# All seven probability slots of a pair by DMA transpose from the eleventh pair on, the scale of v taken in its cast, and half-folded squares on GpSimd

## The chip, the core and the metric

The kernel runs on one NeuronCore of a Trainium2 chip. The core has five engines that run their own instruction streams: TensorE (PE, matrix products; its weight loads, PEld, overlap it), VectorE (DVE), ScalarE (ACT), GpSimd (POOL) and SyncE (SP, which issues the DMAs here). They meet only in semaphores. Operands lie in SBUF; matrix products go to PSUM, eight banks of 512 f32 per partition. The metric is the device time of one execution in microseconds (us).

## What is computed

Attention with RMS-normalised q and k over 8 batches of 12 heads (448 positions, 64 features a head), and then a gated feed-forward block with a three-tap convolution along the sequence:

```python
q_n, k_n = rmsnorm(q, g_q), rmsnorm(k, g_k)
scores = q_n @ k_n.T / sqrt(64)
attn = exp(scores - max(scores)); attn = attn / (sum(attn) + 1e-9)
x = (attn @ v), heads side by side            # 8 x 448 x 768
h = relu(x @ w_in)                            # 768 -> 1024
c = conv3(h, conv_w)                          # along the sequence, per feature
out = (h * sigmoid(c)) @ w_out                # 1024 -> 768
```

## The kernel before

**Pairs.** The unit of attention is a pair of heads (`n`, 0 to 47, six to a batch). Its two heads of 448 rows make 896 query rows, cut into seven **slots** of 128; `SLOTS` gives the order in which they are done, and `GROUPS` joins them for `scores`. A pair passes these steps, each a small function that issues one or a few instructions:

- `load_k`, `load_q` (lines 329 to 338), `square` (340), `square_sum` (349), `rsqrt` (362, nine small steps for two pairs at once), `apply_rms` (396), `qk_transpose` on PE (408), and `qk_hi`, `qk_lo` (419, 427), which split a value into two f16 parts, high and rest.
- `scores` (532) on PE with three f16 products, `soft_max` (545, the row maximum, DVE), `soft_exp` (551, ACT, with the row sums).
- The probabilities have to be turned, so that the keys lie on the partitions. There are two ways. **By PE**: `p_transpose` (582, four transposes of f32) into PSUM and `p_evac` (589, ACT or DVE) out of it into an f32 part of the tile `PT`. **By DMA**: `p_hi` (560) and `p_lo` (568) split the slot into two f16 parts in a buffer `ph`, and `p_turn` (575) is one DMA transpose of both into an f16 part of `PT`. `nd(n)` (516) says how many slots go by DMA: none for the pairs 0 to 7, four (slots j = 0 to 3) for the others.
- `v_load` (461), `v_bound` (466, the largest absolute value), and once for a batch `v_max` to `v_scale` (476 to 493), a power of two by which v is scaled. `v_scaled` (631) multiplies the tile v by it in place. Where slots go by DMA, `v_hi` and `v_lo` (637, 640) split v into two f16 parts.
- `pv` (652) multiplies: the f32 part with four passes over k for both heads (line 660), and the f16 part with three products (line 669). `pvs(n)` lists its pieces.
- The row sums: `sum_step` (596), `sum_transpose`, `sum_evac`, `sum_store` to DRAM and `sum_load` back, spread over 64 partitions; `x_scale` (674) multiplies the PV by them; `x_hi`, `x_lo` split the result for the next product.

**The feed-forward block** of a batch: `in_part` (736) on PE, `in_relu`, `in_conv` (three), `in_tanh`, `in_gate`, `in_hi`, `in_lo`, `in_carry`, and `out_part` (798) on PE, `out_evac`, `out_store`. It is worked into the attention of the next batch, so that PE has products to do while a pair waits for its softmax.

**Order.** Nothing is scheduled on the chip. `plan_*` give each step a due time (`at`), `needs` (915) what it must follow, and `options` (1167) the engines that may do it, with a cost. A list scheduler (1269 to 1396) walks through these and writes out a single order; each engine runs its share of that order from first to last. The constants `PH` (20) shift due times and set how patient a step is with its second engine. `SHARED` (1316) names steps whose DVE form is costed higher when POOL is busy. SP issues all DMAs in one order, loads, sums, turns and stores alike.

**Buffers** (`BUFS`, 104): three of `ph`, two of `PT`, three of `e` (the exponentials), twelve of `x`, eight of `v`.

Of the kernel before, what the change touches and what calls it, by code (L numbers as in the profile page):

```python
# [9 lines left out]
F16 = mybir.dt.float16  # L10
# [10 lines left out]
    T0=18.19, N0=5, T=16.2, ti=26.477, si=4.987, so=6.734, hop=0.568, beta=0.028, wi0=-41.512,  # L21
    wi1=117.871, wo0=38.32, wo1=142.628, cw=-29.146, p_evac=1.158, p_hi=2.093, p_lo=3.44,
    p_rms=1.831, p_v=1.927, p_x=0.005, p_g=2.46, p_relu=0.434, p_cv=1.228, p_qz=1.0, p_ev=8.316,
    sp=0.107, nbulk=5, p_rs=0.005, p_sq=0.882, p_w=0.5, v0=-5.896, dg=2, n1=8, sw=0, pvs=2,
    ct=1.5, p_vs=0.938, p_ph=0.39, p_pl=0.493,
# [23 lines left out]
def tile_attention_moe(ctx: ExitStack, tc, q, k, v, g_q, g_k, w_in, conv_w, w_out, out):  # L49
# [298 lines left out]

    def square_sum(n):
        m = duo(n)[0]  # L350
        nc.vector.tensor_reduce(  # L351
            old("st", m)[:, 0, n - m].rearrange("p i s -> p (i s)"),
            old("sq", n).rearrange("p i h t d -> p (i h t) d"), axis=AX.X, op=ALU.add,
        )
# [273 lines left out]
    def pvs(n):  # L628
        return (*range(0, NB, PV_STEP), *(range(NB, NB + 3) if nd(n) else ()))

    def v_scaled(n):
# [1 line left out]
        elementwise(on["v_scaled", n]).tensor_scalar(  # L633
            v, v, old("vsc", n // NP)[:PB, 1:2], None, op0=ALU.mult
        )
# [793 lines left out]
```

## Time and profile before

| | |
|---|---|
| median of three runs | 978.2 us (975.87 to 981.03) |
| the profiled execution | 978.28 us, span 976.5 us |
| mean granted TensorE clock | 0.962 |
| q1, all DMAs that the kernel issues | 259664 packets, 109.82 MB, 52.1% of 16 engines' span |
| p_turn | 160 DMA transposes |

The page's first part gives busy time, share of the span and number of instructions of each engine; its second part cuts the span into 40 equal slices, each digit being tenths of the slice (9 is 90% or more). A group's row reads: line, engine, operation, written tile <- read tiles, shapes, count | busy time, mean ns of one | idle time ahead of it and what ended it. In a row of the timeline the first number is the start in us and the second the duration; matrix products are pipelined, so the start of the next row tells more than the duration. Many helper functions issue for several steps (line 77 a copy or cast, line 81 a scaled one on ACT, line 89 an operation on two tiles): there, the tile's name tells the step.

### The profile page before, as it was taken

How to read it: one execution, taken by the hardware profiler on the slowest of the kernel's cores; microseconds unless marked ns; L12 is line 12 of the kernel's file. 1: busy time of each engine (PE TensorE's matmuls, PEld its weight loads, DVE VectorE, ACT ScalarE, POOL GpSimd, SP SyncE). 2: the span in 40 equal slices, each digit the busy share in tenths (PEclk: the TensorE clock that was granted, in tenths of full speed). 3: DMA queues.
4: the chain of work that ended last, by engine and by line, in shares of the span. 5: the costliest groups of instructions: out<-in, count | busy, mean ns of one | idle time of the engine just before them, and what ended most of it. 6: DMA issues, size and time to landing. Idle time of an engine off the chain costs nothing.

```text
span 976.5 us, 18886 instructions
## 1 busy us (share of the span) xinstructions
PE 893.8 (92%) x6590; PEld 522.6 (54%) x6590; DVE 777.3 (80%) x1349; ACT 680.4 (70%) x1564; POOL 660.1 (68%) x723
## 2 busy tenths in 40 slices
PE   1777688978999799999999999999999999999988
PEld 0344344545656366655665566556665665556545
DVE  6999979899689967699789977898889966992540
ACT  3678667776666777679688776788788776785331
POOL 2489868886687758498688767587778864772120
PEclk9788669998999999999999999999999999999999
DMA  9945423343773677555765667446684565244001
GB/s 215 247 105 148 126 57 76 64 101 71 155 160 75 107 125 149 116 110 103 153 133 122 125 133 148 102 92 139 144 163 92 109 148 100 51 94 107 17 16 50
DMA packets 259759, 111.02 MB, mean 114 GB/s; under 512 B 220928, under 2 KB 256080, under 8 KB 259664
## 3 DMA queue, kind: packets, MB, share of 16 engines
q1 hardware_dynamic: 259664, 109.82, 52.1%
q8 instruction: 52, 0.85, 0.3%
q14 instruction: 43, 0.35, 0.1%
HBM read 56.65 MB, written 11.18 MB: 69 GB/s over the span
## 4 chain that ended last, share of the span: by engine, by line
PE 49%; DVE 12%; POOL 6%; issue 3%; ACT 3%; DMA 1%; SPq 0%; POOLq 0%; ACTq 0%; DVEq 0%
POOL ph L89 1%; POOL gring L89 1%; POOL sq L89 1%; DMA PT<-ph 1%; DVE st L351 1%; DVE ph L89 1%; POOL x L89 1%; POOL st L386 1%; DVE c_(1_4_3520 L763 0%; POOL st L375 0%; DVE carry L788 0%; PE m_('o'_7_0_0_12066 L812 0%; PE m_('o'_5_3_0_10563 L812 0%; PE m_('o'_3_3_0_7531 L812 0%; PE m_('o'_1_3_0_4495 L812 0%
## 5 line engine op out<-in xcount | busy, mean ns | idle before, releaser
L742 PEld LDWEIGHTS <-wi 128*128 128x128 f16 x1152 | 108.7, 98 | 99.8 <-issue 16.6
L812 PEld LDWEIGHTS <-gring 128*128 128x128 f16 (+1 forms) x1056 | 101.3, 100 | 66.4 <-issue 16.9
L89 POOL TENSOR_TENSOR sq<-qkf,st 112x512 f32<-112x512 f32 x80 | 96.0, 1214 | 2.8 <-ACT wi L254 1.0
L89 POOL TENSOR_TENSOR x<-rB,x 128x448 f16<-128x448 f32 x48 | 57.2, 1191 | 49.3 <-ACT x L77 39.5
L633 POOL TENSOR_SCALAR v<-v,vsc 112x512 f32<-112x512 f32 x42 | 72.0, 1718 | 17.8 <-DVE vsc L186 16.1
L543 PEld LDWEIGHTS <-qT 64*128 64x128 f16 x864 | 32.5, 96 | 71.1 <-issue 55.5
L351 DVE TENSOR_REDUCE st<-sq 112x16 f32<-112x1024 f32 x48 | 58.0, 1209 | 3.2 <-ACT sq L345 2.4
L669 PEld LDWEIGHTS <-vp 112*64 112x64 f16 x960 | 51.1, 110 | 9.7 <-issue 7.8
L441 POOL COPY qz<-qT 64x128 f16<-64x128 f16 x90 | 37.4, 416 | 25.8 <-DVE qT L432 23.1
L89 POOL TENSOR_TENSOR vp<-v,vp 112x512 f16<-112x512 f32 x38 | 46.3, 1219 | 8.9 <-ACT vp L77 6.6
L345 ACT ACTIVATE sq<-qkf 112x1024 f32<-112x1024 f32 x33 | 34.9, 1059 | 4.5 <-DMA qkf<-in_q_dram 4.5
L89 POOL TENSOR_TENSOR sq<-qkf 112x1024 f32<-112x1024 f32 x15 | 30.1, 2005 | 4.5 <-PE t_('qk'_7_0_1418 L412 2.3
L471 DVE TENSOR_REDUCE vacc<-v 112x1 f32<-112x512 f32 x48 | 32.2, 671 | 0.3
L77 ACT CAST vp<-v 112x512 f16<-112x512 f32 x36 | 22.2, 618 | 11.4 <-PE m_('v'_18_4614 L669 3.4
L600 DVE TENSOR_SCALAR rsum<-rsum 128x7 f32<-128x7 f32 x48 | 20.8, 432 | 8.2 <-ACT e_(29_6_7231 L555 1.5
L812 PEld LDWEIGHTS <-carry 128*64 128x64 f16 x192 | 20.2, 114 | 10.8 <-issue 4.1
L375 POOL TENSOR_SCALAR st<-st 112x32 f32<-112x32 f32 (+1 forms) x53 | 19.1, 360 | 10.0 <-DVE st L388 4.2
L386 POOL TENSOR_TENSOR st<-st 112x32 f32<-112x32 f32 (+1 forms) x25 | 10.1, 406 | 22.5 <-DVE st L381 19.4
L812 PEld LDWEIGHTS <-wi 128*128 128x128 f16 (+1 forms) x192 | 19.6, 102 | 9.3 <-ACT wi L77 0.5
L788 DVE COPY carry<-gring 128x128 f16<-128x128 f16 x32 | 19.2, 599 | 5.8 <-POOL gring L89 5.8
L543 PEld LDWEIGHTS <-qz 128*128 128x128 f16 x144 | 14.1, 100 | 16.5 <-issue 6.4
L89 DVE TENSOR_TENSOR sq<-qkf,st 112x512 f32<-112x512 f32 x16 | 22.7, 1424 | 0.0
(3733 smaller groups left out, 3134.2 us busy)
## 6 DMA issues: line engine op xcount, KB each, us to landing
qkf<-in_k_dram SPq DMA_DIRECT2D x48, 224.0 KB
qkf<-in_q_dram SPq DMA_DIRECT2D x48, 224.0 KB
v<-in_v_dram SPq DMA_DIRECT2D x48, 224.0 KB
rB<-rd SPq DMA_DIRECT2D x96, 112.0 KB
wo<-in_moe_w_in_dram SPq DMA_DIRECT2D x12, 512.0 KB
gring<-in_moe_w_out_dram SPq DMA_DIRECT2D x16, 384.0 KB
PT<-ph SPq DMA_TRANSPOSE x160
rd<-rT SPq DMA_DIRECT2D x48, 3.5 KB
```

The source lines that it names most:

```text
L77: (nc.scalar.copy if e == "ACT" else elementwise(e).tensor_copy)(dst, src)
L89: elementwise(e).tensor_tensor(dst, a, b, op=op)
L345: nc.scalar.activation(sq, old("qkf", n), AF.Square)
L351: nc.vector.tensor_reduce(old("st", m)[:, 0, n - m].rearrange("p i s -> p (i s)"), old("sq", n).rearrange("p i h t d -> p (i h t) d"), axi ...
L441: e.tensor_copy(z[HALF[h], :, HALF[h]], old("qT", n)[HALF[h], :, t0 : t0 + 64])
L471: nc.vector.tensor_reduce(old("vacc", b)[:PB, i : i + 1], old("v", n).rearrange("p h t d -> p (h t d)"), axis=AX.X, op=ALU.max, apply_abso ...
L543: nc.tensor.matmul(ps[u][:, :S], lhs, kt[r, w], start=(i == 0), stop=(i == 2))
L600: nc.vector.tensor_scalar(r, r, 1e-9, None, op0=ALU.add)
L633: elementwise(on["v_scaled", n]).tensor_scalar(v, v, old("vsc", n // NP)[:PB, 1:2], None, op0=ALU.mult)
L669: nc.tensor.matmul(ps[HALF[h], out[h]], v[:, w, h, k], pt[:PB, a, k, col[h]], start=(i == 0 and k == 0), stop=(i == 2 and k == NB - 1),)
L742: nc.tensor.matmul(ps[:, :S], wi[:, wl, c, fc * P : (fc + 1) * P], old("x", b * NP + c)[:, xl], start=(i == 0), stop=(i == 3 * NP - 1),)
L812: nc.tensor.matmul(ps[p0 : p0 + m, :NO2], g, wo[:, wl, fc, half * NO2 : (half + 1) * NO2], start=(i == 0), stop=(i == 3 * NFC - 1),)
```

## The change

Five things are done together.

1. `nd(n)` is 0 for the pairs 0 to 9 and 7 for all others. From the eleventh pair on every slot goes through `p_hi`, `p_lo` and `p_turn`; `p_transpose` and `p_evac` are left to the first ten pairs. `pv` is then three f16 products 448 columns wide, with no f32 part. 266 turns take the place of 160. `ph` has four buffers and `x` eleven.
2. `v_scaled` is gone. `v_hi` multiplies by the scale in its cast, `v_lo` is one DVE instruction (product and subtraction), and in the first ten pairs `x_scale` multiplies by the scale too.
3. `square_fold`: in the first 15 pairs POOL adds the upper halves of the 64 squares of a row to the lower halves, and `square_sum` reduces 32 instead of 64.
4. Order: `p_turn` of a pair's first slot follows the pair before, `qk_transpose` follows the scores of two pairs earlier, and between some DMAs (`LOOSE`) the scheduler keeps the order but counts no waiting time. The due times are worked out by a loop and not by recursion.
5. The constants `PH` have other values, so the written order differs everywhere.

```diff
-    T0=18.19, N0=5, T=16.2, ti=26.477, si=4.987, so=6.734, ...
-    sp=0.107, nbulk=5, ..., v0=-5.896, dg=2, n1=8, sw=0, pvs=2,
+    T0=15.375, N0=5, T=16, ti=25.974, si=4.835, so=7.981, ...
+    sp=0.134, nbulk=5, ..., v0=4.399, nd=[7, 7], n1=10, nf=15, sw=0,
...
-        ... e=3, PT=2, x=12, c=3, ... ph=3, vp=2,
+        ... e=3, PT=2, x=11, c=3, ... ph=4, vp=2,
...
+    def square_fold(n):
+        x = old("sq", n).rearrange("p i h t d -> p (i h t) d")
+        binary("POOL", x[:, :, : D // 2], x[:, :, : D // 2], x[:, :, D // 2 :], ALU.add)
+
     def square_sum(n):
...
-            old("sq", n).rearrange("p i h t d -> p (i h t) d"), axis=AX.X, op=ALU.add,
+            x[:, :, : D // 2] if folded(n) else x, axis=AX.X, op=ALU.add,
...
     def nd(n):
-        return 0 if n < PH["n1"] else 2 * PH["dg"]
+        return 0 if n < PH["n1"] else PH["nd"][n % 2]
...
-    def v_scaled(n):
-        v = old("v", n).rearrange("p h t d -> p (h t d)")
-        elementwise(on["v_scaled", n]).tensor_scalar(
-            v, v, old("vsc", n // NP)[:PB, 1:2], None, op0=ALU.mult
-        )
+    def width(n):
+
+        return S if nd(n) == NS else nd(n) // 2 * P

     def v_hi(n):
-        copy(on["v_hi", n], new("vp", n, [PB, 2, 2, NB, D], F16)[:, 0], old("v", n))
+        copy_scaled(
+            on["v_hi", n], new("vp", n, [PB, 2, 2, NB, D], F16)[:, 0], old("v", n),
+            old("vsc", n // NP)[:PB, 1:2],
+        )

     def v_lo(n):
         vp = old("vp", n)
-        binary(on["v_lo", n], vp[:, 1], old("v", n), vp[:, 0], ALU.subtract)
+        nc.vector.scalar_tensor_tensor(
+            vp[:, 1], old("v", n), old("vsc", n // NP)[:PB, 1:2], vp[:, 0],
+            op0=ALU.mult, op1=ALU.subtract,
+        )
...
     def x_scale(n):
-        t = old("rB", n)
-        nc.vector.tensor_tensor(t, old("m", ("v", n))[:, :S], t, op=ALU.mult)
+        t, ps = old("rB", n), old("m", ("v", n))[:, :S]
+        if nd(n):
+            nc.vector.tensor_tensor(t, ps, t, op=ALU.mult)
+        else:
+            nc.vector.scalar_tensor_tensor(
+                t, ps, old("vsc", n // NP)[:, 1:2], t, op0=ALU.mult, op1=ALU.mult
+            )
...
         elif name == "qk_transpose":
             yield "apply_rms", *a
+            yield "scores", n - 2, NG - 1
...
-            yield (("p_turn", n, a[1] - 1) if a[1] else ("p_evac", n - 1, NS - 1))
+            if a[1]:
+                yield "p_turn", n, a[1] - 1
+            else:
+                yield "p_evac", n - 1, NS - 1
+                yield "p_turn", n - 1, nd(n - 1) - 1
...
-            v_lo=lambda: [pool(1.16), dve(0.62)],
+            v_lo=lambda: [dve(0.69)],
...
-            p_turn=lambda: [("SP", 2.0, ("T", 1))],
+            p_turn=lambda: [("SP", 1.6, ("T", 1))],
...
+    LOOSE = {("p_turn", "p_turn"), ("p_turn", "p_evac"), ("v_load", "v_load"), ("load", "load")} | {
+        ("load_k", "load_q"), ("load_q", "load_k"), ("sum_load", "sum_load")
+    }
...
-            ready[s_].append((end, src))
+            ready[s_].append((0.0 if (step[0], s_[0]) in LOOSE else end, src))
```

More of the change, by code (lines that the diff above doesn't have):

```diff
@@ L20 @@
 PH = dict(
[L21 to L25, printed above, removed]
+    T0=15.375, N0=5, T=16, ti=25.974, si=4.835, so=7.981, hop=0.535, beta=0.028, wi0=-38.253,
+    wi1=117.871, wo0=37.751, wo1=147.083, cw=-34.218, p_evac=1.38, p_hi=2.313, p_lo=4.003,
+    p_rms=4.75, p_v=1.435, p_x=0.152, p_g=0.931, p_relu=0.434, p_cv=0.165, p_qz=1.0, p_ev=8.316,
+    sp=0.134, nbulk=5, p_rs=0.005, p_sq=0.499, p_w=0.5, v0=4.399, nd=[7, 7], n1=10, nf=15, sw=0,
+    pvs=2, ct=1.5, p_vs=0.938, p_ph=0.535, p_pl=0.511, dg=2,
 )
@@ L104, in tile_attention_moe @@
     BUFS = dict(
-        qkf=3, sq=2, st=2, qT=2, kT=2, qz=2, v=8, sst=6, e=3, PT=2, x=12, c=3,
-        rB=2, vacc=2, vsc=4, cwb=3, s=3, t=2, m=3, rd=2, rsum=2, rT=2, mx=10, h=2, ph=3, vp=2,
+        qkf=3, sq=2, st=2, qT=2, kT=2, qz=2, v=8, sst=6, e=3, PT=2, x=11, c=3,
+        rB=2, vacc=2, vsc=4, cwb=3, s=3, t=2, m=3, rd=2, rsum=2, rT=2, mx=10, h=2, ph=4, vp=2,
     )
@@ L594, in p_evac @@
         )
+        if nd(n):
+            copy_scaled(*args, old("vsc", n // NP)[:PB, 1:2])
+        else:
+            copy(*args)
     def sum_step(n, i):
@@ L1057, in needs @@
                 yield "p_turn", n, 0
-        elif name == "v_scaled":
+            else:
+                yield "p_evac", n - 1, NS - 1
+                yield "p_turn", n - 1, nd(n - 1) - 1
+            if nd(n):
+                yield "v_scale", n // NP
+        elif name == "v_hi":
             yield "v_scale", n // NP
-            yield "v_bound", n
-        elif name == "v_hi":
-            yield "v_scaled", n
             yield "pv", n - BUFS["vp"], pvs(n - BUFS["vp"])[-1]
@@ L1157, in needs @@
             yield "out_evac", *a
+    turns = [(n, j) for n in range(NPAIR) for j in range(nd(n))]
     def back(n, g, i, m=NS):
@@ L1242, in tile_attention_moe @@
         qk_hi="hi", apply_rms="rms", x_hi="x", x_lo="lo", in_hi="g", in_lo="g", q_middle="qz",
-        out_evac="ev", v_scaled="vs", v_hi="hi", v_lo="lo", p_hi="ph", p_lo="pl", sum_evac="ev", v_bound="v", rest="w", rsqrt="rs", square="sq", convert="w", in_relu="relu", in_conv="cv", p_evac="evac",
+        out_evac="ev", v_hi="hi", p_hi="ph", p_lo="pl", sum_evac="ev", v_bound="v", rest="w", rsqrt="rs", square="sq", convert="w", in_relu="relu", in_conv="cv", p_evac="evac",
     )
@@ L1249, in takes @@
             return "t"
-        if name in ("in_part", "out_part") and not a[-2] or name == "pv" and not a[-1]:
+        if name in ("in_part", "out_part") and not a[-2] or name == "pv" and a[-1] == pvs(a[0])[0]:
             return "m"
@@ L1283, in enqueue @@
             waiting[e][step] = t + (PH["p_" + PATIENCE[step[0]]] if i else 0.0), c, dma
-    sys.setrecursionlimit(20000)
-    due = {}
-    def urgency(step):
-        if step not in due:
-            due[step] = min(
-                [steps[step][0]] + [urgency(p) - PH["hop"] for p in after.get(step, ())]
-            )
-        return due[step]
+    due, count = {}, dict(left)
+    line = [step for step in steps if not left[step]]
+    for step in line:
+        for p in after.get(step, ()):
+            count[p] -= 1
+            if not count[p]:
+                line.append(p)
+    assert len(line) == len(steps), [x for x in steps if count[x]][:12]
+    for step in reversed(line):
+        due[step] = min([steps[step][0]] + [due[p] - PH["hop"] for p in after.get(step, ())])
+    urgency = due.__getitem__
     LAT = {
@@ L1316, in tile_attention_moe @@
     SHARED = (
-        "in_conv", "in_gate", "apply_rms", "p_lo", "p_hi", "v_lo", "v_hi", "v_scaled", "x_hi", "x_lo",
+        "in_conv", "in_gate", "apply_rms", "p_lo", "p_hi", "v_lo", "v_hi", "x_hi", "x_lo",
         "in_hi", "in_lo", "convert", "rest", "square_sum",
     )
+    LOOSE = {("p_turn", "p_turn"), ("p_turn", "p_evac"), ("v_load", "v_load"), ("load", "load")} | {
+        ("load_k", "load_q"), ("load_q", "load_k"), ("sum_load", "sum_load")
+    }
     BULK = ("load", "load_k", "load_q", "v_load")
```

40 lines of the change are left out of this document (25 added, 15 removed).

## The prediction

> **What bounds the kernel now.** I read the page first, for each engine's busy time and for the 40 slices.
>
> ```profile
> span 976.5 us, 18886 instructions
> PE 893.8 (92%) x6590; PEld 522.6 (54%) x6590; DVE 777.3 (80%) x1349; ACT 680.4 (70%) x1564; POOL 660.1 (68%) x723
> ...
> PE   1777688978999799999999999999999999999988
> ```
>
> TensorE is the busiest engine by far, and the slices say where: from about the eleventh slice (250 us) to the end it is nearly always at 9. Before that it isn't. So I cut the span where pairs end, and read busy time by stretch. The rows that mark a pair's end are those of its f16 PV matmuls.
>
> ```profile
> L669 PE MATMUL m_('v'_10_2577<-PT,vp x24: 272/273/297, 248.7 to 250.0; 112*64 112x256 f16 x24
> ...
> L669 PE MATMUL m_('v'_18_4614<-PT,vp x24: 272/272/273, 393.0 to 394.2; 112*64 112x256 f16 x24
> ```
>
> ```profile
> 604.19 1.48 PE L669 MATMUL m_('v'_30_7640<-PT,vp 112*64 112x256 f16 x24
> ```
>
> ```profile
> 47.30:144.50 97.20, 74.96 (x379) 38.96 (x379) 89.70 (x164) 70.54 (x174) 80.30 (x64) 0.75 0.41 110
> 144.50:248.70 104.20, 93.29 (x621) 50.53 (x620) 93.87 (x153) 77.77 (x176) 80.33 (x81) 0.95 0.37 79
> 248.70:392.00 143.30, 135.87 (x1087) 81.13 (x1087) 115.25 (x210) 102.65 (x239) 104.84 (x110) 0.99 0.65 129
> 392.00:603.00 211.00, 207.74 (x1661) 125.64 (x1659) 176.41 (x301) 163.08 (x374) 158.21 (x182) 1.00 0.61 123
> ```
>
> The columns are stretch, length, busy PE, weight load, DVE, ACT, POOL, granted clock, DMA share, GB/s. There are two regimes. Up to 248.7 DVE is busy 92% and 90% and PE has 33 us idle: DVE sets the pace there. From 392 PE is busy 98.5% at clock 1.00, and twelve pairs (v_18 to v_30) take 604.2 - 393.0 = 211.2 us, **17.6 us a pair**. DVE takes 176.4/12 = 14.7 us of those, ACT 13.6, POOL 13.2. So what a pair takes from PE is worth its full length only until DVE becomes the bound at not much less.
>
> **The change part by part.** PE first, from its timeline in a settled stretch; the start of the next row ends a step.
>
> ```profile
> 501.25 0.60 PE L585 MATMUL t_('p'_25_4_6157<-ident,e_(25_4_6148 128*112 128x128 f32 x4
> 501.69 0.73 PE L543 MATMUL s_(25_6_6163<-kT,qz 128*128 128x448 f16 x3
> ...
> 506.74 0.36 PE L543 MATMUL s_(26_0_6222<-kT,qT 64*128 64x448 f16 x1
> ...
> 506.94 0.35 PE L543 MATMUL s_(26_0_6222<-kT,qT 64*128 64x448 f16 x1
> ...
> 512.37 1.52 PE L660 MATMUL m_('v'_25_6305<-PT,v 112*64 112x192 f32 x16
> 513.83 0.74 PE L742 MATMUL m_('i'_3_2_6242<-x,wi 128*128 128x448 f16 x3
> ...
> 518.01 1.50 PE L669 MATMUL m_('v'_25_6305<-PT,vp 112*64 112x256 f16 x24
> 519.45 0.74 PE L742 MATMUL m_('i'_3_3_6324<-x,wi 128*128 128x448 f16 x3
> ```
>
> A p_transpose is 501.69 - 501.25 = 0.44 us; three go per pair, 1.32. The PV is 1.46 (f32) + 1.44 (f16) = 2.90. Afterwards it is 24 f16 matmuls of 448 columns, which run two at a time. From both sides: two matmuls of 448 columns follow each other by 0.20 in the scores, so 12 x 0.20 = 2.4; scaled from the 256-column PV, 1.44 x 448/256 = 2.5. I take 2.4, the row with the same width, and gain 0.50. **PE: 1.82 us a pair**, for pairs 10 to 47. Pairs 8 and 9 go the other way: four p_transposes more, 1.76, and an f32 PV of 448 columns (1.46 x 448/192 = 3.4) for 2.9: 2.3 each, in a stretch where PE has idle time, so 0 to 4.5 in all.
>
> Now the other engines.
>
> ```profile
> L633 POOL TENSOR_SCALAR v<-v,vsc 112x512 f32<-112x512 f32 x42 | 72.0, 1718 | 17.8 <-DVE vsc L186 16.1
> L351 DVE TENSOR_REDUCE st<-sq 112x16 f32<-112x1024 f32 x48 | 58.0, 1209 | 3.2 <-ACT sq L345 2.4
> ...
> L89 POOL TENSOR_TENSOR vp<-v,vp 112x512 f16<-112x512 f32 x38 | 46.3, 1219 | 8.9 <-ACT vp L77 6.6
> ...
> L471 DVE TENSOR_REDUCE vacc<-v 112x1 f32<-112x512 f32 x48 | 32.2, 671 | 0.3
> ```
>
> ```profile
> L89 POOL TENSOR_TENSOR sq<-qkf,st 112x512 f32<-112x512 f32 x80 | 96.0, 1214 | 2.8 <-ACT wi L254 1.0
> ```
>
> ```profile
> L77 ACT CAST ph<-e_(8_0_1778 x1: 565/565/565, 176.6 to 176.6; 128x448 f16<-128x448 f32 x1
> L89 POOL TENSOR_TENSOR ph<-e_(8_0_1778,ph x1: 1031/1031/1031, 177.6 to 177.6; 128x448 f16<-128x448 f32 x1
> ```
>
> ```profile
> 433.47 0.67 DVE L430 SCALAR_TENSOR_TENSOR kT<-t_('qk'_22_1_5057,G,kT 128x448 f16<-128x448 f32 x1
> ```
>
> ```profile
> 554.19 1.89 POOL L89 TENSOR_TENSOR sq<-qkf 112x1024 f32<-112x1024 f32 x1
> ...
> 554.55 2.02 DVE L89 TENSOR_TENSOR ph<-e_(28_3_6867,ph 128x448 f16<-128x448 f32 x1
> ...
> 556.81 0.59 ACT L77 COPY PT<-t_('p'_28_4_6943 112x512 f32<-112x512 f32 x1
> ```
>
> Per pair from the eleventh on: three p_evac (0.59, ACT) become three p_hi (0.565): nothing. Three p_lo are added: 3 x 1.03 = +3.1, mostly POOL. v_scaled goes: -1.72 x 42/48 = -1.5, POOL. v_lo leaves POOL (-1.22) for DVE. On DVE no row shows it with a scale; the same operation on 448 columns took 0.67, so 0.67 is the low end, and 2.02 the high end (a two-input DVE row that lies beside a POOL row); I take 0.7, by the row that is the same operation. POOL comes out at 13.2 + 3.1 - 1.5 - 1.2 = 13.6, ACT unchanged at 13.6. DVE is 14.7 + 0.7, and its share of the added p_lo comes on top; the order can put casts that DVE does now on ACT, which has room. I take **15.2**, between 14.7 and 15.8.
>
> DVE can't be filled: in the two early stretches, where it set the pace, it was busy 92% and 90%. 15.2/0.92 = **16.5 us a pair**, against PE's 17.6 - 1.8 = 15.8. That is the step I choose: the gain is cut off at DVE, at 1.1 and not 1.82. From pair 11 to 47 that is 37 x 1.1 = -41.
>
> Early pairs: folding replaces a reduce of 1.21 on DVE by one of half the size (0.67, the row of that size), and puts one addition of 512 elements on POOL, 1.21. Some 12 of the 15 lie before 248.7: DVE -6.5, and at 91% busy -7 us of time. POOL gets 12 x 1.21 = 14.5 and loses ten v_scaled (-17) and eight p_lo (-8), which covers it; without that cover POOL's 80 us of 97 would grow by 8 in each stretch. With pairs 8 and 9 on PE between 0 and +4.5, I take -6 for the stage, bounds -12 and +3.
>
> The queues. Each p_turn is one more instruction on SP.
>
> ```profile
> L577 SPq DMA_TRANSPOSE PT<-ph x160: 1231/1240/2233, 178.6 to 894.1; - x160
> ```
>
> ```profile
> 434.39 0.58 SPq L619 DMA_DIRECT2D rB<-rd  x1
> ...
> 435.70 3.26 SPq L577 DMA_TRANSPOSE PT<-ph  x2
> ```
>
> ```profile
> 430.08 4.85 DMA PT<-ph
> ...
> 534.30 1.81 PE m_('i'_3_6_6549 L742 x9
> ...
> 641.85 2.41 DMA PT<-ph
> ```
>
> ```profile
> SPq L577 <- POOL ph L89: 75.0, 45, 6.1
> ```
>
> ```profile
> 187.00:190.00 3.00, 3.00 (x22) 1.63 (x17) 2.58 (x5) 1.72 (x4) 2.94 (x3) 1.00 1.11 241
> ```
>
> SP: 7 x 1.24 = 8.7 us a pair, and about six plain issues of up to 0.58, 3.5: 12.2 of 16.5. It fits, but SP is in order and already waits 75.0 us for p_lo; the loads of q, k, v and of the sums queue behind a waiting turn, and x_scale waits for the sums. Bytes: 123 GB/s x 211 us / 12 = 2.16 MB a pair; a turn moves 128 x 1024 f16 = 0.26 MB, so 2.95 MB. At the 241 GB/s of a stretch full of transposes that is 12.2 us of 16.5. Hidden, with less room: the share of 0.61 grows to 0.85 or more. The fourth buffer of ph costs nothing where it is spare. The eleventh (no longer twelfth) x makes the last pair of a batch wait for the batch before it to leave in_part: i_3_6 is at 534, batch 4's last pair just ahead of v_30 at 604, so it is free. The loop for due times and the LOOSE set add no instruction; they only change the order.
>
> The tail is the same work: after the last pair 8 in_part groups and 8 out_part groups of batch 7. I count +1 there for the longer path through the DMA. **Sum**: the profiled execution took 978.28 around its span of 976.5, against the median of 978.2, so nothing is to be scaled: 978.3 - 41 - 6 - 1 + 1 = **931**, where the -1 is the folding of the last pairs.
>
> **The rivals.** *PE stays the bound.* For it: PE is at 98.5%, and DVE's casts can move to ACT. Against it: DVE would be at 15.2/15.8 = 96%, which no stretch shows. 37 x 1.82 = 67, and 7 early: **904**.
>
> *DVE is held up by POOL.* The DVE row at 554.55 starts beside the POOL row at 554.19 and ends 0.49 us after it; the like operation at 433.47 takes 0.67. If more p_lo on POOL make DVE 15.8 a pair, it is 15.8/0.92 = 17.2: 37 x 0.4 = 15, and 5 early: **958**. The Trainium skill (SBUF — State Buffer, "SBUF: two separate sides") has the port pair that the two share as an exclusive lock held for a whole instruction; the two rows agree.
>
> *The turns become the bound: slower.* Four ph buffers carry seven slots; a slot holds one for p_hi 0.57, p_lo 1.03, about 0.3 of hops and the landing L. A pair takes 7/4 x (1.9 + L). With the chain's 2.41 and 4.85 that is 7.5 and 11.8, harmless; it passes 17.6 from L = 8.2 us on. With DMA at 0.85 and SP in order that is possible: at L = 8.8 a pair takes 18.7, 37 x 1.1 = +41, less 7: **1012**. The Trainium skill (VectorE: DVE Perf Modes, "The three transpose paths") gives 1309 ns for a 128x128 transpose by DMA and 390 ns by TensorE. Taken block by block, a turn's eight blocks would be 10.5 us, an estimate by that page; the rows above (two turns issued in 3.26, landing in 2.41) speak against taking it so.
>
> *No effect*: another chain (in_conv to in_gate, the sums' round trip) holds the pair at 17.6: **974**.
>
> **How the numbers follow.** Forecast 931 (915 to 947): 0.52. PE bound, 904: 0.20. DVE held up, 958: 0.14. No effect, 974: 0.06. Turns bind, 1012: 0.08. The range 898 to 962 takes in the first three, with the bounds of v_lo and of the early stage, and leaves out 0.14 to 0.2. A measurement of this kernel tells about 0.5% (5 us) from no change. Faster 0.86, same 0.06, slower 0.08.
>
> **What would show it.** Right: twelve late pairs in about 198 us; no p_transpose after pair 9; PE at 93 to 97% there and DVE above 90%; 266 turns, DMA share about 0.85, and L577's landing under 6 us. Wrong: PE still at 98% (904); DVE rows of twice their length beside POOL (958); p_hi waiting for a turn, or SP's waits for p_lo doubled with PE at 90% or less and its clock under 1.00 (1012). The weakest step is the 92% at which I cut DVE off.

## The result, and the profile after

The changed kernel took **990.38 us** (median of three, 989.2 to 992.46) against 978.2: ratio **1.0128 [1.0093, 1.0164]**. It is slower, where 931 was forecast. The profiled execution took 992.46 around its span. First the page of the changed kernel: busy times, and three lines of its 40 slices.

```profile
span 990.7 us, 17102 instructions
...
PE 854.0 (86%) x5510; PEld 437.6 (44%) x5510; DVE 835.5 (84%) x1383; ACT 693.0 (70%) x1592; POOL 663.2 (67%) x714
...
PE   1768678998997799979997799979997799979988
...
DVE  5899997999889988999789978998799978993450
...
PEclk9988778998999899998999899989999899989999
```

TensorE has lost 40 us of work (893.8 to 854.0), as the change promised. But the span didn't follow: where the slices of PE were 9 in a row, 7s stand among them now, and its clock falls off with them. DVE went the other way, 777.3 to 835.5. Next the rows that end three pairs, from the timeline of the changed kernel (and the row after one of them).

```profile
394.68 2.25 PE L690 MATMUL m_('v'_18_4490<-PT,vp 112*64 112x448 f16 x22
...
614.49 2.46 PE L690 MATMUL m_('v'_30_7314<-PT,vp 112*64 112x448 f16 x24
616.88 0.82 PE L837 MATMUL m_('o'_3_3_1_7357<-wo,gring 128*128 128x384 f16 x4
...
833.84 2.46 PE L690 MATMUL m_('v'_42_10111<-PT,vp 112*64 112x448 f16 x24
```

Twelve pairs take 617.0 - 396.9 = 220.0 us and then 219.3: **18.3 us a pair**, against 17.6 before and 16.5 forecast. From such rows (start and duration added) one sees where the 14.2 us of the two spans arose:

| end of | before | after | after - before |
|---|---|---|---|
| v_11 | 267.7 | 265.9 | -1.8 |
| v_18 | 394.5 | 396.9 | +2.4 |
| v_30 | 605.7 | 617.0 | +11.3 |
| v_42 | 817.5 | 836.3 | +18.8 |
| v_47 | 903.9 | 920.1 | +16.2 |
| span | 976.5 | 990.7 | +14.2 |

So it is lost in the settled stretch, pair after pair. There the busy times of the engines, 24 pairs of the kernel before and then of the changed one (stretch, length, PE, PEld, DVE, ACT, POOL, granted clock, DMA share, GB/s):

```profile
393.00:817.00 424.00, 417.87 (x3346) 253.12 (x3342) 356.77 (x611) 327.77 (x752) 318.70 (x367) 1.00 0.60 125
```

```profile
395.00:834.00 439.00, 393.18 (x2652) 198.58 (x2648) 394.59 (x641) 336.32 (x774) 323.54 (x351) 0.95 0.83 164
```

PE gives back 24.7 us of work in 24 pairs and idles for 46. POOL, ACT and the DMAs (0.83; 0.85 was forecast) are where the prediction had them. DVE is not: 356.77/24 = 14.87 us a pair became 394.59/24 = **16.44**, with only 5% more instructions. At 90% of the pair's 18.3 it is as busy as PE at its lower clock, and its busy time is the one that grew. The chain of waits points the same way, but its shares on the two pages have to be read with care. The kernel before, then the changed one:

```profile
PE 49%; DVE 12%; POOL 6%; issue 3%; ACT 3%; DMA 1%; SPq 0%; POOLq 0%; ACTq 0%; DVEq 0%
```

```profile
PE 22%; DVE 15%; issue 3%; ACT 3%; POOL 3%; POOLq 0%; DVEq 0%; ACTq 0%
```

The shares are of the whole span, but the chain that the profile could follow starts only at 248 us in the kernel before and at 521 us in the changed one; so they add up to 74% and 46% and can't be set side by side. Its pieces from 530 us to the end of v_42, which both have, can: there DVE has 14% of the stretch before and 38% after, PE 69% and 43%. And SP's waits for p_lo did nearly double (us, count, longest), as the rival of the turns asked:

```profile
SPq L587 <- POOL ph L88: 143.0, 99, 13.3
```

So at this point there were four theories: **(A)** DVE has more work of its own (v_lo above all); **(B)** DVE is held up by POOL, which now does twice as many p_lo; **(C)** the turns bind; **(D)** the written order itself is worse.

### The profile page after: what moved, and what is told of

It is laid out like the page before. It is cut to its first block, busy times and chain, and to the rows that moved or that the text cites. A ratio compares the mean times of both kernels' runs of the same rounds, so it can differ in the third digit from the quotient of the medians.

```text
span 990.7 us, 17102 instructions
## 1 busy us (share of the span) xinstructions
PE 854.0 (86%) x5510; PEld 437.6 (44%) x5510; DVE 835.5 (84%) x1383; ACT 693.0 (70%) x1592; POOL 663.2 (67%) x714
## 5 line engine op out<-in xcount | busy, mean ns | idle before, releaser
L88 POOL TENSOR_TENSOR sq<-qkf,st 112x512 f32<-112x512 f32 x91 | 110.4, 1229 | 4.7 <-DVE st L381 2.3
L355 DVE TENSOR_REDUCE st<-sq 112x16 f32<-112x1024 f32 (+1 forms) x48 | 49.9, 1043 | 14.0 <-ACT sq L344 12.2
L88 POOL TENSOR_TENSOR sq<-qkf 112x1024 f32<-112x1024 f32 x12 | 23.7, 1978 | 22.1 <-PE t_('qk'_3_0_654 L420 9.1
L660 DVE SCALAR_TENSOR_TENSOR vp<-v,vsc,vp 112x512 f16<-112x512 f32 x38 | 37.9, 996 | 0.5 <-ACT vp L80 0.5
L615 DVE TENSOR_SCALAR rsum<-rsum 128x7 f32<-128x7 f32 x48 | 28.7, 598 | 2.6 <-ACT e_(46_6_10795 L565 0.9
L76 ACT CAST x<-rB 128x448 f16<-128x448 f32 x34 | 19.0, 560 | 12.7 <-DVE rB L698 10.5
L837 PEld LDWEIGHTS <-carry 128*64 128x64 f16 x192 | 21.5, 120 | 13.6 <-issue 5.4
L80 ACT ACTIVATE vp<-v,vsc 112x512 f16<-112x512 f32 x34 | 24.4, 718 | 3.8 <-DVE vsc L185 1.5
L88 POOL TENSOR_TENSOR sq<-sq 112x512 f32<-112x512 f32 x15 | 20.5, 1365 | 9.4 <-ACT sq L344 9.1
L394 DVE TENSOR_TENSOR st<-st 112x32 f32<-112x32 f32 (+1 forms) x27 | 20.8, 771 | 4.7 <-POOL st L384 4.2
L381 DVE SCALAR_TENSOR_TENSOR st<-st 112x32 f32<-112x32 f32 (+1 forms) x41 | 21.5, 526 | 2.4 <-POOL st L396 1.1
L553 PEld LDWEIGHTS <-qz 128*128 128x128 f16 x144 | 14.5, 105 | 15.1 <-issue 5.5
```

The costliest lines, as they stand in the source:

```text
L88: elementwise(e).tensor_tensor(dst, a, b, op=op)
L355: nc.vector.tensor_reduce(old("st", m)[:, 0, n - m].rearrange("p i s -> p (i s)"), x[:, :, : D // 2] if folded(n) else x, axis=AX.X, op=AL ...
L381: v.scalar_tensor_tensor(dst, x, c, z, op0=ALU.add, op1=ALU.mult)
L553: nc.tensor.matmul(ps[u][:, :S], lhs, kt[r, w], start=(i == 0), stop=(i == 2))
L615: nc.vector.tensor_scalar(r, r, 1e-9, None, op0=ALU.add)
L660: nc.vector.scalar_tensor_tensor(vp[:, 1], old("v", n), old("vsc", n // NP)[:PB, 1:2], vp[:, 0], op0=ALU.mult, op1=ALU.subtract,)
```

## The experiments

### Which engine or queue binds: four short cuts

Four kernels take one suspect each off the changed kernel; the written order stays the same in all.

`s_vlo`, v_lo as a fill:

```diff
-        nc.vector.scalar_tensor_tensor(
-            vp[:, 1], old("v", n), old("vsc", n // NP)[:PB, 1:2], vp[:, 0], ...
+        nc.vector.memset(vp[:, 1], 0.0)
```

> The changed kernel with its written order, but v_lo is a DVE memset of the same tile, so the low part of v is zero and left out of the product. DVE theory (DVE sets the pace: its rows are longer and it has v_lo on top): v_lo goes from 1.02 us to about 0.15 a pair, 38 x 0.87 = 33 us of DVE, so 990 falls to 955 to 968. Turn theory (the DMA transposes, their landing or SP's order set the pace): 985 to 992. PE theory: 985 to 992.

Measured: 980.15, ratio to before 1.001 [0.9988, 1.0031]. Some 10 us come back, less than A wanted. In its settled pairs DVE has 15.61 us a pair and not 16.44, and the pair takes 18.05 and not 18.31: of 0.83 us taken off DVE, 0.26 come back. Work of DVE counts in part, but v_lo isn't the cause by itself.

`s_turn`, half of each turn (the low part alone is turned, and the PV reads it in place of the high one too):

```diff
-            places(n)[1].rearrange("p a k q -> p (a k) q")[:, :, c * P : (c + 1) * P],
-            old("ph", (n, j)).rearrange("q a k p -> q (a k p)"),
+            places(n)[1][:, 1, :, c * P : (c + 1) * P],
+            old("ph", (n, j))[:, 1].rearrange("q k p -> q (k p)"),
```

> The changed kernel with its written order, but a turn moves only the low part (512 of 1024 columns), and all three PV products read that part; the high part is left out. Turn theory: half the bytes of 266 turns are gone (35 MB), the landing is shorter, 990 falls to 945 to 970. DVE theory: 983 to 992, nothing on DVE has changed.

Measured: 990.35, ratio 1.012 [1.0072, 1.0168]. The time stays: the bytes of the turns don't set it. The windows of this run:

```profile
397.00:836.00 439.00, 393.29 (x2652) 198.10 (x2651) 394.23 (x639) 335.86 (x773) 322.39 (x351) 0.95 0.50 113
```

`s_pv`, the third product of the PV left out:

```diff
         i = k0 - NB
+        if i == 2:
+            return
...
-                    start=(i == 0 and k == 0), stop=(i == 2 and k == NB - 1),
+                    start=(i == 0 and k == 0), stop=(i == 1 and k == NB - 1),
```

> The changed kernel with its written order, but the third PV product (low part of the probabilities with the high part of v) is left out from the eleventh pair on: PE has 0.8 us a pair less, 30 us in all. PE theory: 958 to 965. DVE theory and turn theory: 983 to 992.

Measured: 986.01, ratio 1.0076 [1.0052, 1.0101]. A third of the PV's work on PE, 30 us by the estimate above, is worth 4 us, and the interval overlaps that of the changed kernel. PE isn't the bound.

`s_plo`, p_lo on one of its four blocks of keys:

```diff
-            on["p_lo", n, j], ph[:, 1, :, :PB], ...
+            on["p_lo", n, j], ph[:, 1, :1, :PB], ...
```

> The changed kernel with its written order, but p_lo does only a quarter of its columns (the low part is left out for the rest; the buffers are zeroed once at the start). POOL's p_lo falls from 1.13 to about 0.35 us, 5 us of POOL a pair. DVE theory with the port as its cause (DVE rows of two tiles wait behind POOL): the in_conv rows fall from 1.05 back towards 0.68 and the time to 945 to 970. If the turns' path through POOL and SP is the bound: 945 to 970 as well, but with in_conv rows still near 1.0. If DVE's own work is the bound and not the blocking: 980 to 992.

Measured: **935.13**, ratio 0.9555 [0.9513, 0.9598]: 55 us back, and on the place of the forecast. The windows over its 24 pairs (17 us a pair, from the ends of v_18 and v_42):

```profile
380.80:786.90 406.10, 385.57 (x2655) 196.44 (x2654) 327.16 (x640) 331.79 (x773) 215.71 (x351) 0.97 0.89 177
```

DVE's busy time fell by 67 us (394.59 to 327.16) with the same 640 instructions. Of 168 p_lo 154 are on POOL; those that DVE has were cut to a quarter too, which is 8 of the 67 us. So either POOL's 108 us less (323.54 to 215.71) were the bound, or DVE's own rows became shorter because POOL worked less beside them. s_plo doesn't tell these two apart.

### Is it POOL's time, or what POOL reads?

Here POOL is kept busy by instructions that read no tile: p_lo is done on 8 columns, and fills stand for the rest. DVE's p_lo are untouched.

```diff
+        if on["p_lo", n, j] == "POOL":
+            binary("POOL", ph[:, 1, :1, :8], ev[:, :1, :8], ph[:, 0, :1, :8], ALU.subtract)
+            for i in range(3):          # s_pmem; range(2) in s_pmem2
+                nc.gpsimd.memset(ph[:, 1, 1:, :PB], 0.0)
+            return
```

> The changed kernel with its written order, but where POOL has p_lo, it subtracts 8 columns only and then fills the rest with three memsets of 336 columns, so that POOL is held for about as long (1.2 us against 1.13) and the turn waits as before; the low part is left out for the other columns. Port theory (DVE's rows wait while POOL reads two tiles): a memset reads nothing, so the in_conv rows fall to about 0.8 and the time to 935 to 955, though POOL is as busy. POOL theory (POOL's own length, or the way of a slot through it to the turn, sets the pace): 985 to 997.

Measured: 962.82, ratio 0.9829 [0.9808, 0.985], between the two ranges, with POOL busier than in the changed kernel:

```profile
388.30:809.60 421.30, 388.38 (x2653) 197.88 (x2653) 335.67 (x640) 333.49 (x773) 349.45 (x812) 0.97 0.87 171
```

> As the run with three memsets in place of POOL's p_lo, but with two, since three held POOL 1.5 us a slot and not 1.2. Two hold it for about 1.1, as p_lo does. Port theory: POOL leaves the chain, DVE's rows stay short: 938 to 955. POOL theory: 960 or more.

Measured: **937.35**, ratio 0.9577 [0.956, 0.9594].

```profile
375.50:784.40 408.90, 386.26 (x2653) 196.18 (x2653) 333.31 (x640) 333.07 (x773) 295.84 (x658) 0.97 0.89 176
```

POOL's rows on the tile ph sum up to 171.7 us in the 24 pairs of the changed kernel (154 slots, 1.115 each), to 148.4 here (0.97 a slot) and to 208.3 in s_pmem (1.36). A p_lo that nothing disturbs takes 1.03. The two runs thus lie on both sides of the true length, and a straight line between them gives 942 us at 1.03 and 947 at 1.115. That is an estimate: at equal time on POOL, **43 to 48 us of the 990 come from what p_lo reads**, not from how long it runs. DVE is at 14.0 and 13.9 us a pair in these two runs, whatever POOL's length. In the chain of s_pmem2, from 510 us to the end of v_42, DVE is back at 12% and PE at 76%. The groups of DVE show it row by row; first the changed kernel over 396 to 836, then s_pmem2 over 380 to 800, about its 24 pairs (busy time, mean ns of one | idle time before):

```profile
L355 DVE TENSOR_REDUCE st<-sq 112x16 f32<-112x1024 f32 x24 | 28.9, 1210 | 10.1 <-ACT sq L344 10.0
L660 DVE SCALAR_TENSOR_TENSOR vp<-v,vsc,vp 112x512 f16<-112x512 f32 x24 | 24.4, 1015 | 0.0
L615 DVE TENSOR_SCALAR rsum<-rsum 128x7 f32<-128x7 f32 x25 | 18.3, 731 | 1.4 <-ACT e_(37_6_8698 L565 0.3 <-ACT e_(25_6_5889 L565 0.3 <-ACT e_(40_6_9437 L565 0.2
...
L394 DVE TENSOR_TENSOR st<-st 112x32 f32<-112x32 f32 x13 | 11.5, 883 | 3.3 <-POOL st L384 3.1
L381 DVE SCALAR_TENSOR_TENSOR st<-st 112x32 f32<-112x32 f32 x21 | 11.3, 539 | 1.8 <-POOL st L396 1.1 <-POOL st L384 0.3
```

```profile
L355 DVE TENSOR_REDUCE st<-sq 112x16 f32<-112x1024 f32 x25 | 30.2, 1214 | 12.5 <-ACT sq L344 12.5
L663 DVE SCALAR_TENSOR_TENSOR vp<-v,vsc,vp 112x512 f16<-112x512 f32 x24 | 18.6, 776 | 0.1
L381 DVE SCALAR_TENSOR_TENSOR st<-st 112x32 f32<-112x32 f32 x21 | 7.5, 355 | 3.6 <-POOL st L396 2.4 <-POOL st L384 0.7
L618 DVE TENSOR_SCALAR rsum<-rsum 128x7 f32<-128x7 f32 x24 | 6.1, 255 | 0.8 <-ACT e_(39_6_9616 L565 0.4 <-ACT e_(40_6_9825 L565 0.2
L394 DVE TENSOR_TENSOR st<-st 112x32 f32<-112x32 f32 x13 | 4.7, 365 | 4.0 <-POOL st L384 3.8
```

The reduction keeps its 1.21 us. v_lo goes from 1015 to 776 ns, and a product on 32 columns from 883 to 365: tiny instructions that wait inside their own rows. The addition on seven columns (L618 here) has 255 ns; in the changed kernel it has 731 and is the costliest of the small ones. It was slowed before as well, only less; the same group over the 24 pairs of the kernel before:

```profile
L600 DVE TENSOR_SCALAR rsum<-rsum 128x7 f32<-128x7 f32 x24 | 10.6, 442 | 4.8 <-ACT e_(29_6_7231 L555 1.5 <-ACT e_(41_6_10267 L555 1.3 <-ACT e_(24_6_5969 L555 0.3
```

How it happens can be read in its timeline (start, duration, engine, line):

```profile
530.72 2.42 POOL L88 TENSOR_TENSOR sq<-qkf,st 112x512 f32<-112x512 f32 x2
...
531.16 1.08 DVE L798 SCALAR_TENSOR_TENSOR c_(3_3_6071<-c_(3_3_6071,hbuf 128x448 f32<-128x448 f32 x1
...
532.17 2.45 DVE L788 SCALAR_TENSOR_TENSOR c_(3_4_6162<-hbuf,cwb,c_(3_4_6162 128x448 f32<-128x448 f32 x1
...
533.11 1.03 POOL L88 TENSOR_TENSOR ph<-e_(27_0_6199,ph 128x448 f16<-128x448 f32 x1
...
534.10 1.41 POOL L88 TENSOR_TENSOR ph<-e_(27_1_6225,ph 128x448 f16<-128x448 f32 x1
534.54 1.45 DVE L88 TENSOR_TENSOR ph<-e_(26_6_6133,ph 128x448 f16<-128x448 f32 x1
...
535.91 0.61 DVE L557 TENSOR_REDUCE sst_(27_2_6246<-s_(27_2_6213 128x1 f32<-128x448 f32 x1
...
536.56 0.64 ACT L565 ACTIVATE e_(27_2_6252<-s_(27_2_6213,sst_(27_2_6246 128x448 f32<-128x448 f32 x1 [2.57 <-DVE sst_(27_2_6246 L557]
```

The tap of in_conv at 532.17 starts beside a product on POOL and lasts 2.45 us until p_lo of slot 0 is done as well; its undisturbed length is 0.67. Then DVE's own p_lo takes 1.45 beside POOL's. The row maximum of slot 2, which is short and undisturbed, comes only at 535.91, and the exponential on ACT has waited 2.57 us for it: that is how DVE's wait gets into the chain. The longest tap of the changed kernel, at 422.38, took 3.44 us, through three such operations of POOL in a row. Rows of DVE in the 24 pairs, sorted by what POOL does at their start (mean us; in brackets the number of rows; "two tiles" are POOL's TENSOR_TENSOR of any size, "POOL idle" is both kernels together, and a row that starts so can still be caught later):

| DVE row | POOL idle | beside POOL, two tiles: before | after |
|---|---|---|---|
| second and third tap of in_conv, 128x448 | 0.70 (44) | 1.08 (34) | 1.24 (40) |
| in_gate, 128x448 | 0.61 (23) | 0.92 (12) | 1.10 (22) |
| rsum + 1e-9, 128x7 | 0.16 (21) | 0.80 (9) | 1.12 (14) |
| v_lo, 112x512 | 0.74 (4) | - | 1.03 (18) |
| sum of squares, a reduction from SBUF | 1.21 (17) | 1.20 (4) | 1.21 (12) |
| row maximum, from PSUM | 0.61 (106) | 0.61 (91) | 0.61 (97) |
| kT's rest, from PSUM | 0.67 (11) | 0.68 (17) | 0.68 (17) |

POOL's TENSOR_SCALAR v_scaled, which reads one tile, is another case. From the kernel before:

```profile
503.25 1.56 POOL L633 TENSOR_SCALAR v<-v,vsc 112x512 f32<-112x512 f32 x1
...
504.22 0.62 DVE L600 TENSOR_SCALAR rsum<-rsum 128x7 f32<-128x7 f32 x1
...
504.30 0.68 DVE L763 SCALAR_TENSOR_TENSOR c_(3_0_6188<-hbuf,cwb,c_(3_0_6188 128x448 f32<-128x448 f32 x1
```

Beside it DVE's rows of two tiles kept their length in the 24 pairs: two taps took 0.68, five p_lo 0.63 (0.62 undisturbed). Rows of one tile did not: both rsum that started beside it took 0.62 or 0.63 in place of 0.16, up to its end. The change took this mild instruction away from POOL and put harmful ones in its place, at nearly equal busy time of POOL. It also moved POOL's v_lo (22 rows of two tiles in the 24 pairs) to DVE.

The same exchange in the kernel **before**, which has 78 p_lo on POOL in 24 pairs and not 154, with two fills (`b_pmem2`, the edit above):

> The kernel before with its written order, and POOL's p_lo (3.25 a pair) replaced by 8 columns of it and two memsets, as in the changed kernel's run; the low part is left out for the other columns. If PE sets the pace there and the port costs it little: 965 to 978. If the port costs the kernel before as much for each p_lo as the changed one (53 us for 6.4 a pair): 945 to 960.

Measured: 967.69, ratio 0.9871 [0.9836, 0.9906].

```profile
391.10:809.80 418.70, 415.69 (x3326) 252.68 (x3328) 335.11 (x611) 327.30 (x752) 300.75 (x523) 1.00 0.61 126
```

DVE is relieved there too, from 14.87 to 335.11/24 = 13.96 us a pair, but PE is at 99% and only 12 us come of it (the kernel before took 979.85 beside it). What p_lo holds up costs 12 us at most where PE is the bound, and over 40 in the changed kernel. And between b_pmem2 and s_pmem2, with p_lo harmless in both and each in its own written order, the change is worth 967.69 - 937.35 = **-30 us**, and still some -20 with the 947 that the straight line gives for fills as long as p_lo. With p_lo as it is, the same two orders are 12 us apart the other way.

### Undoing one part of the change

`u_nd4`: four slots by DMA again, the rest of the change kept.

```diff
-    ... nd=[7, 7], n1=10, nf=15, ...
+    ... nd=[4, 4], n1=10, nf=15, ...
```

> The changed kernel with one part undone: four slots by DMA from the eleventh pair on, three by PE, written order made anew. The scale in the cast, the folding and the other constants stay. Port theory: POOL's two-tile rows are 8.7 us a pair against 10.0 before and 12.0 after, so DVE is freer than in the kernel before and PE, with its old length, sets the pace again: 960 to 978. Theory that the new order or the constants cost the time: 985 to 995.

Measured: 992.92, ratio 1.0136 [1.0111, 1.0161]: not what the port theory expected, but in the range of the theory that the order or the constants cost the time. Its windows:

```profile
385.50:826.60 441.10, 421.54 (x3328) 251.77 (x3328) 370.41 (x610) 326.69 (x745) 295.50 (x346) 0.99 0.58 120
```

DVE is relieved (15.4 us a pair), PE has its work again at 96%, and the time is as before the undoing. PE with 421.54 of work can't be much below 424, but here it is at 441. A planned kernel is planned anew when a part of it changes, with constants that were chosen for another plan: this run can't carry a verdict on the turns, and neither can the next two on their parts alone. Hence the control with the new rules and none of the work, further down.

`u_v`: v_scaled in place again, v_hi and v_lo without a scale, v_lo on POOL or DVE.

```diff
+    def v_scaled(n):
+        v = old("v", n).rearrange("p h t d -> p (h t d)")
+        elementwise(on["v_scaled", n]).tensor_scalar(
+            v, v, old("vsc", n // NP)[:PB, 1:2], None, op0=ALU.mult
+        )
...
-            v_lo=lambda: [dve(0.69)],
+            v_scaled=lambda: [pool(1.5), dve(0.4)],
+            v_lo=lambda: [pool(1.16), dve(0.62)],
```

> The changed kernel with another part undone: v is scaled in place (v_scaled, mostly POOL) and v_lo may go to POOL again; all slots by DMA, written order made anew. Theory that v_lo on DVE is the main cost: DVE loses 1.0 us a pair, 960 to 975. Port theory: POOL gets 2.5 us a pair more (1.1 of them a two-tile row) and has 16 of 18 us to do; DVE's rows stay long: 985 to 1010.

Measured: 991.76, ratio 1.0125 [1.0104, 1.0147]: the same as the changed kernel, in another written order. That v_lo on DVE is the main cost is not borne out; what it costs on DVE, held up, against POOL, where it holds up others, this run can't separate from the order.

`u_fold`: no folding (`nf=15` becomes `nf=0`).

> The changed kernel without the folding (no pair folded), written order made anew. If the folding pays in the early stage, where DVE is at 97%: 993 to 1000 (DVE 15 x 0.5 us more). If its two-tile row on POOL takes back what it gives: 986 to 993.

Measured: 983.55, ratio 1.0044 [1.0017, 1.0071]. **Without the folding the kernel is 7 us faster**; both ranges on record lie above this time. v_10 ends at 238.8 without it, at 248.7 with it (at 244.7 to 246.7 in s_turn, s_vlo and s_pv, whose first ten pairs are the same), and the settled pairs take the same (18.35 and 18.31 us), so the gain lies where the folding was. But the written order is another one too, and how much of the 7 us is the order stays open. The windows of the early stage, first the changed kernel, then u_fold:

```profile
100.00:150.00 50.00, 35.27 (x177) 17.49 (x174) 49.51 (x79) 34.42 (x81) 37.69 (x29) 0.76 0.38 102
```

```profile
100.00:150.00 50.00, 35.28 (x180) 18.02 (x180) 47.15 (x88) 33.46 (x81) 36.67 (x37) 0.76 0.35 93
```

DVE is at 99% with folding, and does 79 instructions in the time in which it did 88 without: 627 ns each against 536, though its reductions were halved. What the fold does on POOL is the page's row:

```profile
L88 POOL TENSOR_TENSOR sq<-sq 112x512 f32<-112x512 f32 x15 | 20.5, 1365 | 9.4 <-ACT sq L344 9.1
```

It is an addition of two tiles, the kind beside which DVE's rows stretch. It saves DVE half a reduction, which nothing on POOL holds up; that it takes this back by holding up DVE's other rows fits these windows, but no run with the order kept shows it.

### Building up from the kernel before

The control `p_base` has all parts of the change undone and the constants and buffers of the kernel before; only the new rules of order (point 4) are left in.

```diff
-    T0=15.375, N0=5, T=16, ..., nd=[7, 7], n1=10, nf=15, ...
+    T0=18.19, N0=5, T=16.2, ..., nd=[4, 4], n1=8, nf=0, ...
...
-        ... x=11, ... ph=4, ...
+        ... x=12, ... ph=3, ...
```

> A control: the code of the changed kernel with all parts undone and the constants and buffers of before (four slots by DMA from pair 8 on, v scaled in place, no folding); what is left of the change are the rules of order (point 4). If these rules cost nothing: 973 to 984. If they cost what was lost: 985 to 995.

Measured: **997.01**, ratio 1.0187 [1.0166, 1.0207]. The same steps as in the kernel before, in another written order (and a few on another engine), take 18 us more; PE has the same work (892.7 us against 893.8).

`p_vonly` is the control with the scale taken in the cast:

> The control with the scale of v taken in its cast, nothing else. Port theory: v_scaled (one tile read, no wait for DVE) is gone from POOL and v_lo (1.0 us) is on DVE; PE sets the pace at 17.6, so 970 to 982. Theory that v_lo on DVE is what costs: 985 to 1000.

Measured: 997.68, ratio 1.0198 [1.0178, 1.0217]; against the control +0.7, nothing.

`p_turns` is the control with all seven slots by DMA from the eleventh pair on, and the new buffers:

> The control with all seven slots by DMA from the eleventh pair on and the changed kernel's buffers, nothing else. POOL gets 3.3 us a pair more of p_lo and has v_scaled and v_lo besides, 16 of 17.6 us. Port theory: DVE's rows and POOL's load both hold the pair above 18: 990 to 1015. My forecast's reading (DVE at 15 us a pair, PE shorter): 925 to 950.

Measured: 1006.61, ratio 1.0291 [1.0267, 1.0315]; against the control **+9.6**, in the range of the port theory and far from the forecast's. But this order is made anew as well, and 9.6 us are no more than an order is worth here: that the turns alone make the kernel slower is not shown by this run.

`p_all` is the changed kernel with the constants of the kernel before:

> The changed kernel with the constants of before (written order made anew; slots, scale, folding and buffers as changed). If the constants are worth little: 987 to 997. If the order that they write matters as in the control: 1000 to 1025.

Measured: 1002.31, ratio 1.0237 [1.0204, 1.0269]. The new constants are worth 12 us to the changed kernel.

`p_noloose` is the control with an empty set LOOSE:

> The control (rules of order alone, constants of before) with the set LOOSE empty, so that the scheduler counts the waiting times between DMAs again. If LOOSE is what costs the control its 18 us: 974 to 984. If it is the other rules, or any new order under constants that were not chosen for it: 988 to 1002.

Measured: 1016.38, ratio 1.0377 [1.0353, 1.0402]. That is above both ranges. LOOSE is not what costs the control its 18 us; without it it is 19 slower still. Which of the other rules does it stays open. D is thus partly borne out: the order moves this kernel by 10 to 20 us either way, though it explains nothing of s_pmem2, whose order is that of the changed kernel.

### Relieving DVE without leaving anything out

If DVE's rows that POOL holds up set the pace, they should be moved to ACT, which has nearly a third of its time free. `c_act` is u_fold with two such rows moved; the order is that of u_fold:

```diff
-            nc.vector.tensor_scalar(r, r, 1e-9, None, op0=ALU.add)
+            nc.scalar.activation(r, r, AF.Copy, bias=1e-9)
...
-        nc.vector.tensor_copy(carry[:, b // 2 % 2, :, fc], ...
+        nc.scalar.copy(carry[:, b // 2 % 2, :, fc], ...
```

> The changed kernel without folding, in the written order that gave 983.5, but the first sum_step (0.72 us a pair on DVE, 0.16 of it work) and in_carry (0.31) are done by ACT in the same places. DVE theory: 1.0 us of DVE a pair less, as with v_lo taken out (-10 us): 970 to 976. If DVE does not set the pace: 980 to 987.

Measured: 973.84, ratio 0.9932 [0.991, 0.9954], so -9.7 against u_fold.

`b_act` is the kernel before with the same two rows moved:

> The kernel before in its written order with the same two steps on ACT. PE sets the pace there: 972 to 980. If DVE's waiting already costs it: 962 to 970.

Measured: 983.63, ratio 1.004 [1.0018, 1.0062]: slightly slower, above both ranges. Where PE is the bound, this relief for DVE brings nothing.

`c_act2` is c_act with the squares of the rsqrt that DVE had, all p_hi and the first tap of in_conv on ACT too:

```diff
+            if e == "DVE":
+                nc.scalar.activation(t, y, AF.Square)
...
-            on["p_hi", n, j], ph[:, 0, :, :PB],
+            "ACT", ph[:, 0, :, :PB],
...
-            copy_scaled(on["in_conv", b, fc, i], c, ...
+            copy_scaled("ACT", c, ...
```

> As c_act, and in the same places ACT also does the squares inside rsqrt that DVE had (0.48 us a pair), and all casts p_hi (0.34) and first in_conv steps (0.25) that DVE had. Another 1.0 us a pair off DVE, 0.7 on ACT. DVE theory: 958 to 968. If ACT or POOL has become the bound by then: 970 to 980.

Measured: **967.89**, ratio 0.9871 [0.9854, 0.9887]. It leaves nothing out, and it beats the kernel before by 1.3% and the changed one by 22 us, of which 16 come from the moved rows (from 983.55) and the rest from u_fold. Its page:

```profile
span 966.4 us, 17002 instructions
...
PE 845.1 (87%) x5510; PEld 436.0 (45%) x5510; DVE 776.6 (80%) x1226; ACT 717.8 (74%) x1737; POOL 647.0 (67%) x710
```

DVE is back at the 777 us that it had before the change. The settled pairs are not faster than then (381.7 to 812.3 from v_18 to v_42, 17.9 us a pair); the gain lies ahead of them, where DVE set the pace before, too: v_18 ends at 381.7 and not at 394.5. The forecast's 931 it doesn't reach: p_lo on POOL still stands beside DVE's rows, and the 45 taps of its 24 pairs that start beside a two-tile operation take 1.30 us each.

## Why the prediction was wrong, point by point

**PE's gain: right.** The p_transposes are gone after the tenth pair, and the PV takes 616.88 - 614.49 = 2.39 us (2.4 forecast). PE's busy time fell by only 24.7 us in 24 pairs, where 1.82 a pair would be 44; but it ran at a clock of 0.95 and not 1.00, and 393.18 x 0.95 = 373.5 is 44 less than 417.87: 1.85 a pair at full clock (an estimate that takes busy time as the inverse of the clock; s_plo gives 385.57 x 0.97 = 374.0). So where PE idled, part of its gain went into its lower clock.

**POOL, ACT, SP and the DMAs: right.** POOL at 13.5 us a pair (13.6 forecast), ACT at 14.0, the DMA share at 0.83 (0.85). The turns' bytes don't count: s_turn halves them and keeps the time.

**DVE as the engine that cuts the gain off, at 90 to 92%: right as far as it goes. Its size: wrong, and this is the step that failed.** "I take **15.2**, between 14.7 and 15.8." It was 16.44; at 90% that is the measured 18.3, and 18.3 - 16.5 = 1.8 us over the 24 settled pairs alone is 43 of the 59 us by which the forecast missed. The prediction put v_lo's 0.7 on DVE and took some of its casts away, and this sum of work was even a little high: with p_lo made harmless, DVE has 13.96 us a pair in the kernel before (b_pmem2) and 13.89 in the changed one (s_pmem2). DVE got **hardly any more work** (with each row at its undisturbed length 13.3 and 13.6 us a pair, an estimate). What grew is what p_lo on POOL adds to DVE's rows: 14.87 - 13.96 = 0.91 us a pair before, 16.44 - 13.89 = 2.55 after. The p_lo on POOL became twice as many (78 to 154 in 24 pairs), their cost on DVE 2.8 times as large. In the forecast's sum the 0.91 was hidden in the 14.7, and no term let it grow. The price of v_lo has the same flaw in small: 0.7 was read from a row with an operand in PSUM (0.67 at 433.47), a kind that POOL doesn't hold up, while v_lo took 0.74 undisturbed and 1.02 on average.

That the two runs with p_lo harmless end near 931 is in part luck. In the 24 settled pairs s_pmem2 takes (784.4 - 375.5)/24 = 17.0 us and s_plo 16.9, not 16.5, with DVE at 81% and PE at 94 to 95%: neither DVE at 92% (13.89/0.92 = 15.1) nor PE's 15.8 gives that. They gain 14 and 17 us in these pairs, where 26 were forecast, and 28 and 25 outside of them, where 21 were. What holds the settled pairs at 17 there stays open.

**The rival "DVE is held up by POOL" had the mechanism and the wrong price.** It gave 15.8 a pair and 958 us. It had one pair of rows for its price (2.02 against 0.67) and counted it on few of DVE's instructions; the traces show it on taps, gates, products, casts and copies from SBUF to SBUF, the tiny ones most of all by ratio, and not on the reductions, the reciprocal (0.19 beside POOL as alone) or rows with an operand in PSUM. The range's upper end was set by this price and so was short.

The Trainium skill (SBUF — State Buffer, "SBUF: two separate sides") says that the pair of ports which the two engines share is an exclusive lock: the one that starts first has it for its whole instruction, and the other one blocks. The trace agrees for POOL's operations on two tiles (taps of 0.67 undisturbed take 1.24, 3.44 at the worst) and for its fills, beside which 28 taps of s_pmem2 took 0.67. The same sentence counts any GpSimd operation that reads SBUF against a DVE operation with two SBUF inputs; beside the one-tile v_scaled two taps kept their 0.68 and five p_lo 0.63, so there the measurement decides.

**The early stage: too much, and the folding in it wrong in sign as far as the runs tell.** -6 was forecast, and v_10 ends 1.5 us earlier; in u_fold, without the fold and in its own order, it ends 11 earlier (250.2 before, 238.8). "Folding replaces a reduce of 1.21 on DVE by one of half the size": the reduction is of the kind that POOL doesn't hold up.

**"They only change the order": wrong.** p_base shows 18 us for the new rules under the old constants, and p_all 12 us for the constants in the changed kernel. The order isn't the cause of the sign: in the same two written orders the change is worth -20 to -30 us once p_lo is harmless. But a forecast that puts it at nothing has a range too narrow by it.

**The turns as the bound: fell.** SP's waits for p_lo doubled as this rival said, and PE fell to 90% with its clock under 1.00, which the prediction had listed as its signs. They were signs of something else. s_turn halves the bytes and keeps the time, and s_pmem2 has all 266 turns at full size and takes 937.35, with SP waiting no less for POOL's rows on ph (fills come last in them):

```profile
SPq L590 <- POOL ph L584: 136.7, 109, 4.3
```

A long wait of a queue doesn't tell what it costs, nor what made it long.

**PE stays the bound, and no effect: both fell.** PE is busy 90% of the settled pairs, a third of the PV less is worth 4 us (s_pv), and a pair takes 18.3 us, neither 15.8 nor 17.6.

What stays open: which rule of order costs the control its 18 us, what the folding and the turns cost with the order kept, what holds the settled pairs at 17 us once p_lo is harmless, and how the 43 to 48 us are to be set against the order, since each replanned kernel lies somewhere between 983 and 1016.

## What to carry to other kernels

In a kernel like this one, count POOL's two-tile instructions on SBUF as work of DVE, too, as soon as DVE is near the bound: split the rows of DVE in the trace by what POOL does at their start, and use the mean beside POOL for all that the change adds there. Moving work between engines at equal busy time isn't neutral when the kind of instruction changes: on POOL, one that only writes was free for DVE's large rows, one that reads a single tile held up only DVE's rows of one tile, and one that reads two held up both. And in a kernel with a planned order, a control with the new rules and none of the work belongs beside every comparison, since the order alone was worth 18 us here. Where that is as much as the effect, keep the order and change one instruction in its place, as the runs with fills do.
